# GpSimd's decay of the last two heads' state over 120 partitions instead of 80

## The chip, the cores and the metric

The kernel runs on one core of a Trainium2 chip. The metric is the device time of one execution in microseconds (us). A core has five engines that run side by side, each through its own list of instructions in order: TensorE (PE in the profile, with PEld for its weight loads), VectorE (DVE), ScalarE (ACT), GpSimd (POOL) and SyncE (SP, which here only issues transfers). On-chip memory (SBUF) has 128 partitions, and an instruction works on the same stretch of each partition that it covers. "80x82" in the profile means 80 partitions with 82 elements in each.

## What is computed

Two parts, one after the other. First a recurrent attention (an mLSTM cell) over 4 batches, 8 heads, 768 steps and head width 40, with a matrix state C and a vector state n for each head:

```python
m_new = np.maximum(f_gate[:, :, t] + m, i_gate[:, :, t])
f_stab = np.exp(f_gate[:, :, t] + m - m_new)
i_stab = np.exp(i_gate[:, :, t] - m_new)
C = f_stab * C + i_stab * outer(vt, kt)
n = f_stab * n + i_stab * kt
y[:, :, t] = sigmoid(o_gate) * (C @ qt) / max(|n . qt|, 1)
```

Then a gated feed-forward on the 3072 rows of 320 numbers that come out: `(sigmoid(x @ w_gate) * (x @ w_val)) @ w_out`, with an inner width of 1536. All data are float32.

## The kernel before

**Units.** The 768 steps are cut into 6 chunks of 128. A unit n = 4c + b is one chunk c of one batch b; there are 24. A unit loads q, k, v and the output gate, turns q and k, computes scores inside the chunk (L749 and its like), multiplies them by a matrix of decays (L868), sums over the values (L929, from unit 8 on with the decays split into three bfloat16 parts, L883 and L887 on GpSimd), and adds what the state of the chunks before gives (matmul L913, scaled at L918).

**The state.** `cst` holds C and n of all heads between chunks: 128 partitions, then batch, then 3 groups of heads, then 123 columns. Groups 0 and 1 hold three heads each (3 x 40 = 120 partitions, 3 x 41 = 123 columns); group 2 holds the last two heads (80 partitions, 82 columns). After a chunk, `cd` multiplies the state by the chunk's decay (L1039, on GpSimd), `cm` brings the chunk's own sum from PSUM to a temporary tile (L1056, ScalarE), and `ca` adds that to the state (L1061, VectorE). Each of the three is there twice for a unit: `.0` for groups 0 and 1 together (120x246) and `.1` for group 2 (80x82). `cd` and `ca` exist for chunks 1 to 4, so 16 of each form run. `cdec` holds the decays, with one value for each partition, chunk, batch and group. For chunk 0, `cm` writes into `cst` itself.

**The feed-forward** is cut into 103 pieces: matmuls into two PSUM tiles pg (L1080, L1084, L1085), tanh on ScalarE (L1090, `th`), gate times value on VectorE (L1097, `gx`), a split of the result into two parts (L1102 on ScalarE, L1107 on VectorE), and the output matmuls (L1117 to L1119). These pieces are mixed with the units so that TensorE has work throughout.

**What sets the order.** The list ORDER (L46 to L192) names every operation once; they are issued in that order, and each engine takes its own in that order. Waits between engines are semaphores that the framework puts in. So an engine whose next instruction can't go on holds back all that are behind it in its list.

**GpSimd's other work** around the change: L659 (a difference of decays, 128x1024), L667 (a causal mask, `affine_select`, 128x1024), L883 and L887 (the splits), L877 (k times decay), L896 and L901 (the split of v), L1018 (the low part of x). At the start it clears and fills constant tiles (L331 to L354, and the identity). VectorE's instructions with two inputs in SBUF are `ca` (L1061), `sl` (L729, on stacks of q and k, 126x1024), L976 and L527; those of L1097, L1107, L918 and L941 have one input in PSUM.

Of the kernel before, what the change touches and what calls it, by code (L numbers as in the profile page):

```python
# [13 lines left out]
ALU = mybir.AluOpType  # L14
# [29 lines left out]


ORDER = """  # L46
    lo0 wz il lf i1 wdo0 li lq0 wdv0 lk0 tab pz wdr0 wao0 i0 lk1 og0 i3 i2 ga lq1 gm0 gb sp1.1 sp0.1 tap wav0 wbo0
    wco0 woo0 gs0 war0 tr0.1 wk0 tac cp0.1 wbr0 sp1.0 tr0.0 ee1.1 sp0.0 wdo4 gc lk2 wcr0 wbv0 wk1 wk2 lv0 ld2 tr1.0
    lv1 ee0.1 cp0.0 tr1.1 ee0.0 wk3 cp1.0 lq2 wk4 l10 wdg0 wor0 s0.0 wk5 kw0 gm1 wcv0 whr0 wov0 gm2 cp1.1 t0.1 s1.0
    t0.0 who0 wk6 tr2.1 wlr0 av0 l11 gm3 ee1.0 whv0 kw1 t1.1 wlo0 t1.0 lo1 tr2.0 cp2.1 nd0 av1 ns0 cs0 wdo1 ee2.0  # L50
    ee2.1 lq3 ro0 ld3 wk7 wao4 wlv0 cp2.0 nd1 xd0 xt0 wk8 wag0 wbg0 og1 wao1 ns1 xh0 em2 cm0.1 wcg0 ro1 lv2 kw2 wm
    lk3 wbo4 xl0 wog0 xd1 wbo1 cm0.0 wco4 whg0 wdg1 xt1 wco1 xh1 tr3.0 cp3.0 woo4 xl1 u1.0 woo1 wdo3 ee3.1 lo2 gm4
    s2.0 wlg0 t2.0 wdv1 u0.0 who4 wlo4 ee3.0 t2.1 tr3.1 r1.0 cp3.1 tbp lo3 em3 kw3 wag1 wk9 wao3 i8 wbg1 cs1 wdr1
    gs1 cm1.0 tbc wk10 og2 r0.0 l12 wbo3 wk11 wcg1 lk4 who1 av2 wco3 th0 wog1 woo3 gx0 u0.1 whg1 cm1.1 ns2 lv3 wlo1
    r0.1 gh0 nd2 gl0 s3.0 wlg1 wav1 og3 dn0.1 u1.1 wbv1 who3 wcv1 t3.0 wdo5 wov1 war1 lq4 wbr1 ro2 wlo3 lo4 th1 r1.1
    u0.2 dn0.0 wcr1 whv1 wao5 l13 t3.1 gx1 gh1 wor1 wbo5 cs2 wlv1 ld4 av3 wdo2 gm5 whr1 gl1 nd3 cm2.1 dn1.1 cm2.0
    u1.2 ns3 gd wdv3 xd2 tr4.0 xt2 wlr1 wco5 ro3 woo5 r0.2 cp4.0 xd3 xh2 th2 r1.2 tr4.1 wdo10 gx2 dn1.0 xl2 cp4.1
    ee4.1 lq5 u0.3 xt3 gh2 wao2 gl2 og4 wbo2 xh3 r0.3 wdg2 tdp wco2 woo2 th3 i7 who5 xl3 tdc who2 lk5 wlo5 u1.3 r1.3
    wav3 wlo2 gx3 u0.4 tr4.2 r0.4 cs3 th4 cp4.2 dn2.1 gh3 u0.5 wao10 wbv3 gl3 wbo10 u1.4 wco10 dn2.0 ld5 lq6 qb4.1
    wdr2 r1.4 ee4.0 tr5.0 qb4.0 r0.5 wag2 gx4 cm3.1 dn3.0 em4 th5 kw4 dn3.1 gh4 woo10 gl4 wcv3 cm3.0 wov3 who10  # L60
    qb4.2 wbg2 wdv2 u0.6 u1.5 r1.5 dn4.3 cp5.0 whv3 gx5 s4.2 r0.6 wlv3 gh5 t4.2 th6 wdr3 lv4 gl5 in4 s4.0 wcg2 u1.6
    war2 ti4 r1.6 wbr2 wdg3 u0.7 dn4.2 gx6 t4.0 lo6 wlo10 l14 r0.7 wcr2 i6 wav2 gh6 wog2 whg2 wlg2 s4.1 wor2 gl6
    wdg4 cs4 dn5.3 u1.7 wdr4 whr2 r1.7 wlr2 th7 ee5.1 wbv2 wcv2 dn5.2 gx7 t4.1 war3 dn6.3 ee5.0 wbr3 wov2 whv2 gh7
    u0.8 wlv2 wcr3 wor3 av4 gl7 wag3 ld6 r0.8 em5 lk6 u1.8 r1.8 cm4.1 dn7.3 th8 wbg3 og6 cm4.0 ad4 wcg3 tr5.2 war4
    nd4 lv5 ns4 tr6.0 lo7 whr3 cp5.2 dn6.2 wbr4 u0.9 dn7.2 wlr3 tr5.1 gx8 gh8 cp6.0 ee6.1 wdo6 tr6.2 r0.9 gl8 wcr4
    ro4 wor4 qb5.0 wao6 cp5.1 l15 dn8.2 wog3 lv6 wbo6 lq7 u1.9 whg3 cp6.2 tep qb5.2 wlg3 dn8.1 wco6 tr6.1 r1.9 dn8.3
    tec th9 whr4 wdv4 s5.0 cp6.1 gx9 wag4 kw5 gh9 u0.10 qb6.0 wdr5 wbg4 lk7 cd4.1 wcg4 qb5.1 wlr4 gl9 t5.0 in5 ca4.1
    war5 u1.10 r1.10 ti5 cd4.0 ee6.0 dn9.1 r0.10 woo6 wog4 wbr5 th10 dn8.0 dn9.3 lq9 wcr5 s5.1 who6 wlo6 whg4 gx10
    u0.11 wdo8 gh10 wdv5 wav4 wor5 gl10 wbv4 wcv4 dn9.2 t5.1 xd4 qb6.2 wlg4 u1.11 whr5 s5.2 dn10.1 r0.11 em6 th11
    dn10.0 lv7 wov4 t5.2 wlr5 gs2 wdo7 wao8 dn9.0 tr7.0 wao7 whv4 dn10.2 r1.11 wbo8 wlv4 ld7 lo5 u0.12 wco8 gx11  # L70
    gh11 gs3 wbo7 av5 cp7.0 lq8 cs5 gl11 woo8 wav5 ca4.0 og5 ee7.1 dn10.3 wdg5 wbv5 lv8 kw6 u1.12 cm5.1 wco7 cm5.0
    ad5 ns5 who8 nd5 s6.2 woo7 gs5 xt4 wcv5 t6.2 og7 ro5 wlo8 gs4 xh4 r0.12 r1.12 in6 th12 lk8 u0.13 who7 wag5 xl4
    wdo9 qb6.1 wdo11 gx12 xd5 wlo7 wbg5 l17 dn11.1 tr7.2 ti6 gh12 r0.13 cd6.0 tr7.1 dn11.0 wcg5 gl12 wov5 cp7.2
    dn11.2 th13 s6.1 cp7.1 dn12.3 wog5 wao9 whg5 wlg5 l18 s6.0 u1.13 qb7.2 cd5.0 l16 tq8 lq10 whv5 r1.13 cd5.1 u0.14
    gx13 t6.0 ca5.1 t6.1 dn12.1 ca5.0 dn11.3 wlv5 ld8 wbo9 r0.14 dn12.0 wco9 gh13 tw8.0 av6 woo9 tw8.3 dn12.2 gl13
    wao11 who9 ad6 qb7.0 cs6 nd6 th14 wlo9 tw8.1 ee7.0 dn13.0 u1.14 r1.14 ns6 dn13.2 cm6.1 wbo11 gx14 xt5 ld9 gh14
# [127 lines left out]
def mlstm_then_gated_ffn_kernel(  # L204
# [13 lines left out]
    nc = tc.nc  # L218
    B, H, S, D = q.shape
# [7 lines left out]
    DA = D + 1  # L227
# [5 lines left out]
    def E(name, n=None):  # L233
        x = PARAM["eng"].get(name if n is None else f"{name}{n}", PARAM["eng"].get(name, "p"))
        return nc.gpsimd if x == "p" else nc.vector
# [18 lines left out]
    def sbt(tag, shape, dt, name, bufs=1):  # L254
        return sb.tile(shape, dt, tag=turn(tag, bufs), name=name)
# [6 lines left out]
    def op(name):  # L262
        def put(f):
            assert name not in ops, name
            ops[name] = f
            return f
        return put
# [19 lines left out]
    cdec = const.tile([P, NCH, B, 3], F32, name="cdec")  # L287
    cst = const.tile([P, B, 3, 3 * DA], F32, name="cst")
# [6 lines left out]
    @op("wz")  # L295
    def _():
        nc.vector.memset(warm, 0.0)
# [31 lines left out]
    @op("i0")  # L329
    def _():  # L330
        nc.gpsimd.memset(mend[:, 0:1], -1e30)  # L331
        nc.gpsimd.memset(m0, 0.0)

    @op("i1")
    def _():
# [234 lines left out]
    def unit(n):  # L570
        c, b = divmod(n, B)
        t0 = c * L
# [9 lines left out]
        def rows(t):  # L582
            return t[b, :, t0 : t0 + L, :].rearrange("h t d -> t h d")
# [4 lines left out]
        @op(f"lq{n}")  # L588
        def _():
            qt[n] = pads[n][0][:, :, :D] if padded else sbt("q", [P, H, D], F32, f"q_{n}", 3)  # L590
            (nc.scalar if n == 0 else nc.sync).dma_start(qt[n], rows(q))
# [179 lines left out]
        elif not stacked:  # L771
            hl = "hl"[b % 2]

            for g, (h0, nh) in enumerate(GROUPS):
                r = nh * D
# [29 lines left out]
        else:  # L805
            for g, (h0, nh) in enumerate(GROUPS):
                r = nh * D
# [224 lines left out]
        for y, (g0, ng, r, w) in enumerate(((0, 2, 3 * D, 3 * DA), (2, 1, 2 * D, 2 * DA))):  # L1032
            gs = slice(g0, g0 + ng)
            cv = cst[:r, b, gs, :w]

            if c > 0:
                @op(f"cd{n}.{y}")
                def _(cv=cv, gs=gs, r=r, ng=ng, w=w, y=y):
                    E(f"cd{y}", n).tensor_tensor(cv, cv, cdec[:r, c, b, gs].unsqueeze(2).broadcast_to([r, ng, w]), ALU.mult)  # L1039

            if c > 0 and PARAM["CA"]:
                @op(f"ca{n}.{y}")
                def _(cv=cv, gs=gs, r=r, w=w):
                    for j in range(w // DA):
                        js = slice(j * DA, (j + 1) * DA)
                        nc.vector.scalar_tensor_tensor(cv[:, :, js], pc_[n][:r, gs, js], rmask[:r, j : j + 1], cv[:, :, js],
                                                       ALU.mult, ALU.add)
                continue

            @op(f"cm{n}.{y}")  # L1050
            def _(cv=cv, gs=gs, r=r, ng=ng, w=w, y=y):
                tmp = cv if c == 0 else sbt(f"ct{ng}", [P, ng, w], F32, f"ct{ng}_{n}")[:r]
                tmps[y] = tmp
                for j in range(w // DA):
                    js = slice(j * DA, (j + 1) * DA)
                    nc.scalar.activation(tmp[:, :, js], pc_[n][:r, gs, js], AF.Copy, scale=rmask[:r, j : j + 1])  # L1056

            if c > 0:
                @op(f"ca{n}.{y}")
                def _(cv=cv, y=y):  # L1060
                    E("ca", n).tensor_tensor(cv, cv, tmps[y], ALU.add)  # L1061
# [70 lines left out]
    n = 0  # L1132
# [39 lines left out]
```

## Time and profile before

| what | us |
|---|---|
| median of 3 runs | 537.78 |
| lowest and highest of them | 537.2, 539.06 |
| the profiled execution, its own time | 535.29 |
| its span, from the first to the last instruction | 533.6 |
| TensorE busy | 509.8 (96% of the span) |
| VectorE busy | 360.3 (68%) |
| ScalarE busy | 250.6 (47%) |
| GpSimd busy | 240.4 (45%) |

The profile is of one execution. The difference between its own time and its span (1.7 us) lies around the instructions. TensorE's clock was granted in full throughout. Busy shares are means over the whole span: GpSimd's 45% says nothing about whether somebody waits for it in a given stretch. In the rows further down, a line starts with the time of the start and the duration in us; a bracket at its end holds how long the engine sat idle before it and what ended that.

### The profile page before, as it was taken

How to read it: one execution, taken by the hardware profiler on the slowest of the kernel's cores; microseconds unless marked ns; L12 is line 12 of the kernel's file. 1: busy time of each engine (PE TensorE's matmuls, PEld its weight loads, DVE VectorE, ACT ScalarE, POOL GpSimd, SP SyncE). 2: the span in 40 equal slices, each digit the busy share in tenths (PEclk: the TensorE clock that was granted, in tenths of full speed). 3: DMA queues.
4: the chain of work that ended last, by engine and by line, in shares of the span. 5: the costliest groups of instructions: out<-in, count | busy, mean ns of one | idle time of the engine just before them, and what ended most of it. 6: DMA issues, size and time to landing. Idle time of an engine off the chain costs nothing.

```text
span 533.6 us, 10378 instructions
## 1 busy us (share of the span) xinstructions
PE 509.8 (96%) x3637; PEld 465.4 (87%) x3637; DVE 360.3 (68%) x827; ACT 250.6 (47%) x576; POOL 240.4 (45%) x268
## 2 busy tenths in 40 slices
PE   5999999999998998899999889999999999999997
PEld 5889988889998998888888778888788888999996
DVE  6998889867586887667688288857555475753322
ACT  4878766645435454453436352544424333323222
POOL 1566567556508754267546564645350605130000
PEclk9999999999999999999999999999999999999999
DMA  9898887554969777698768775765794515101001
GB/s 214 209 244 242 220 182 202 138 119 97 180 153 197 133 141 145 144 204 184 139 127 196 144 161 135 163 127 125 143 206 86 129 31 136 39 28 41 1 1 50
DMA packets 222476, 74.13 MB, mean 139 GB/s; under 512 B 167380, under 2 KB 214168, under 8 KB 222424
## 3 DMA queue, kind: packets, MB, share of 16 engines
q1 hardware_dynamic: 221336, 73.20, 61.9%
q8 instruction: 29, 0.48, 0.4%
q10 hardware_dynamic: 1088, 0.26, 0.3%
q14 instruction: 23, 0.19, 0.1%
HBM read 61.54 MB, written 11.90 MB: 138 GB/s over the span
## 4 chain that ended last, share of the span: by engine, by line
PE 80%; DMA 8%; DVE 5%; SPq 2%; issue 2%; ACT 1%; POOL 0%; DVEq 0%; ACTq 0%
PE pg L1080 34%; PE po L1117 7%; PE po L1119 6%; PE po L1118 6%; PE pg L1084 6%; PE pg L1085 5%; DMA qs<-scq 3%; PE av L947 3%; PE s L749 2%; PE av L929 2%; PE in L913 2%; DMA scx<-tx 2%; PE cs L1028 2%; PE s L804 1%; DMA xf<-scx 1%
## 5 line engine op out<-in xcount | busy, mean ns | idle before, releaser
L1080 PE MATMUL pg<-xh,wh 128*128 128x256 f32 (+1 forms) x412 | 107.0, 341 | 12.9 <-DVE gl L1107 6.7
L1102 ACT ACTIVATE gh<-pg 128x256 fp32r<-128x256 f32 (+1 forms) x103 | 48.3, 469 | 139.1 <-DVE pg L1097 91.5
L1097 DVE SCALAR_TENSOR_TENSOR pg<-sg,pg 128x256 f32<-128x256 f32 (+1 forms) x103 | 54.8, 532 | 82.7 <-PE pg L1085 54.3
L1080 PE MATMUL pg<-xl,wh 128*128 128x256 f32 (+1 forms) x412 | 101.3, 327 | 0.6 <-POOL xl L1018 0.6
L1080 PE MATMUL pg<-xh,wl 128*128 128x256 f32 (+1 forms) x412 | 101.0, 326 | 0.0
L1117 PE MATMUL po<-oh,gh 128*128 128x320 f32 x288 | 92.4, 321 | 0.1
L1119 PE MATMUL po<-oh,gl 128*128 128x320 f32 x288 | 89.6, 311 | 0.2 <-DVE gl L1107 0.2
L1118 PE MATMUL po<-ol,gh 128*128 128x320 f32 x288 | 89.3, 310 | 0.0
L1080 PEld LDWEIGHTS pg<-xh,wh 128*128 128x128 f32 x412 | 66.8, 189 | 20.3 <-DVE gl L1107 9.3
L1107 DVE TENSOR_TENSOR gl<-pg,gh 128x256 fp32r<-128x256 f32 (+1 forms) x103 | 54.2, 526 | 40.5 <-ACT gh L1102 39.3
L1090 ACT ACTIVATE sg<-pg 128x256 f32<-128x256 f32 (+1 forms) x103 | 48.1, 467 | 64.7 <-PE pg L1085 58.3
L1080 PEld LDWEIGHTS pg<-xl,wh 128*128 128x128 f32 x412 | 68.9, 189 | 8.5 <-POOL xl L1018 1.4
L1080 PEld LDWEIGHTS pg<-xh,wl 128*128 128x128 f32 x412 | 68.9, 189 | 7.2
L883 POOL TENSOR_TENSOR dr<-d 128x1024 f32<-128x1024 f32 x16 | 30.4, 1903 | 97.5 <-DVE d L868 71.9
L1084 PE MATMUL pg<-xh,w 128*128 128x256 f32 (+1 forms) x206 | 69.9, 340 | 0.0
L1085 PE MATMUL pg<-xl,w 128*128 128x256 f32 (+1 forms) x206 | 66.9, 326 | 0.0
L1117 PEld LDWEIGHTS po<-oh,gh 128*128 128x128 f32 x288 | 54.4, 189 | 3.8 <-ACT gh L1102 0.4
L1118 PEld LDWEIGHTS po<-ol,gh 128*128 128x128 f32 x288 | 54.2, 188 | 3.4
L1119 PEld LDWEIGHTS po<-oh,gl 128*128 128x128 f32 x288 | 54.2, 188 | 0.8 <-DVE gl L1107 0.7
L1018 POOL TENSOR_TENSOR xl<-xf,xh 128x384 fp32r<-128x384 f32 x16 | 16.9, 1056 | 56.9 <-ACT xh L1014 49.0
L1085 PEld LDWEIGHTS pg<-xl,w 128*128 128x128 f32 x206 | 39.1, 190 | 2.1
L1084 PEld LDWEIGHTS pg<-xh,w 128*128 128x128 f32 x206 | 39.0, 189 | 2.2
(156 smaller groups left out, 914.8 us busy)
## 6 DMA issues: line engine op xcount, KB each, us to landing
d<-mscr SPq DMA_DIRECT2D x22, 512.0 KB
ks<-scq SPq DMA_DIRECT2D x48, 168.0 KB
qs<-scq SPq DMA_DIRECT2D x48, 168.0 KB
scq<-tq SPq DMA_DIRECT2D x64, 80.0 KB
o<-in_o_gate_dram SPq DMA_DIRECT2D x24, 160.0 KB
su_o<-in_moe_w_out_dram SPq DMA_DIRECT2D x12, 320.0 KB
v<-in_v_dram SPq DMA_DIRECT2D x24, 160.0 KB
out_dram<-ob SPq DMA_DIRECT2D x24, 160.0 KB
```

What stands on the lines that cost most here:

```text
L883: E("da", n).tensor_tensor(dr[n][0], dm[n], top(dm[n]), ALU.subtract)
L1018: (E("xl", n) if xbounced else nc.vector).tensor_tensor(xl[c][:, :, bs], xf[n], xh[c][:, :, bs].bitcast(F32), ALU.subtract)
L1080: nc.tensor.matmul(p, w[y][:, a, fs], x[c][:, a, n0:n1], start=(i + a == 0), stop=False)
L1084: nc.tensor.matmul(pg[n, y], w2[y][:, fs], xh[c][:, 2, n0:n1], start=False, stop=False)
L1085: nc.tensor.matmul(pg[n, y], w2[y][:, fs], xl[c][:, 2, n0:n1], start=False, stop=True)
L1090: nc.scalar.activation(s, pg[n, 0], AF.Tanh, scale=0.5)
L1097: nc.vector.scalar_tensor_tensor(sgs[n], gate, 1.0, pg[n, 1], ALU.add, ALU.mult)
L1102: nc.scalar.activation(ghs[n][:, :nt], sgs[n], AF.Copy)
L1107: E("gl", n).tensor_tensor(gls[n][:, :nt], sgs[n], ghs[n][:, :nt].bitcast(F32), ALU.subtract)
L1117: nc.tensor.matmul(p, ghs[n][:, ts], oh[:, j, :], start=(j == 0), stop=False)
L1118: nc.tensor.matmul(p, ghs[n][:, ts], ol[:, j, :], start=False, stop=False)
L1119: nc.tensor.matmul(p, gls[n][:, ts], oh[:, j, :], start=False, stop=(j == NF - 1))
```

## The change

A new operation `iz` on GpSimd clears partitions 64 to 127 of group 2 in `cst`, for all four batches, once at the start. And `cd`, the decay, works on 120 partitions in both its forms; before, the form of group 2 worked on the 80 that hold data. The rows 80 to 119 of group 2 hold zeros, are multiplied by a decay of zero, and nobody reads them. ORDER gets the name `iz` behind `i0`; its lines are wrapped anew and nothing else in it moves.

```diff
-    lo0 wz il lf i1 wdo0 li lq0 wdv0 lk0 tab pz wdr0 wao0 i0 lk1 og0 i3 i2 ga lq1 gm0 gb sp1.1 sp0.1 tap wav0 wbo0
+    lo0 wz il lf i1 wdo0 li lq0 wdv0 lk0 tab pz wdr0 wao0 i0 iz lk1 og0 i3 i2 ga lq1 gm0 gb sp1.1 sp0.1 tap wav0
...
         nc.gpsimd.memset(mend[:, 0:1], -1e30)
         nc.gpsimd.memset(m0, 0.0)
 
+    @op("iz")
+    def _():
+        nc.gpsimd.memset(cst[64:, :, 2, : 2 * DA], 0.0)
+
...
             if c > 0:
                 @op(f"cd{n}.{y}")
-                def _(cv=cv, gs=gs, r=r, ng=ng, w=w, y=y):
-                    E(f"cd{y}", n).tensor_tensor(cv, cv, cdec[:r, c, b, gs].unsqueeze(2).broadcast_to([r, ng, w]), ALU.mult)
+                def _(gs=gs, ng=ng, w=w, y=y):
+                    cw = cst[: 3 * D, b, gs, :w]
+                    E(f"cd{y}", n).tensor_tensor(cw, cw, cdec[: 3 * D, c, b, gs].unsqueeze(2).broadcast_to([3 * D, ng, w]), ALU.mult)
```

## Rows read from the trace of the kernel before

**Rows 1.** The two forms of L1039 on POOL: busy us, mean ns, idle before.

```profile
L1039 POOL TENSOR_TENSOR cst<-cst,cdec 120x246 f32<-120x246 f32 x16 | 10.7, 667 | 0.1
L1039 POOL TENSOR_TENSOR cst<-cst,cdec 80x82 f32<-80x82 f32 x16 | 5.6, 352 | 7.3 <-PE in L913 7.3
```

**Rows 2.** Timeline of PE, 163 to 176 and 308 to 325 us: its two longest stops.

```profile
173.46 0.50 PE L1080 MATMUL pg<-xh,wh 128*128 128x256 f32 x2 [1.69 <-DVE gl L1107]
...
321.15 0.73 PE L1080 MATMUL pg<-xh,wh 128*128 128x512 f32 x2 [2.79 <-ACT sg L1090]
```

**Rows 3.** The chain that ended last, 160 to 178 and 305 to 325 us: start, us, what.

```profile
169.98 2.13 DVE qs L729
...
318.12 1.27 DVE ks L729
```

**Rows 4.** Timeline of POOL, 308 to 325 us, and its next instruction after that.

```profile
311.65 0.32 POOL L1039 TENSOR_TENSOR cst<-cst,cdec 80x82 f32<-80x82 f32 x1 [1.89 <-PE in L913]
311.93 2.14 POOL L667 TENSOR_SCALAR_AFFINE_SELECT d<-d 128x1024 f32<-128x1024 f32 x2
314.03 1.90 POOL L887 TENSOR_TENSOR ds<-dr 128x1024 bf16<-128x1024 f32 x1
...
316.49 1.44 POOL L877 TENSOR_TENSOR k<-k,d 128x320 f32<-128x320 f32 x2
...
326.61 1.90 POOL L883 TENSOR_TENSOR dr<-d 128x1024 f32<-128x1024 f32 x1 [8.68 <-PE av L929]
```

**Rows 5.** Timeline of DVE, 308 to 325 us: the add of the state, twice.

```profile
312.46 5.74 DVE L1061 TENSOR_TENSOR cst<-cst,ct 120x246 f32<-120x246 f32 x1
...
322.23 0.40 DVE L1061 TENSOR_TENSOR cst<-cst,ct 120x246 f32<-120x246 f32 x1
```

**Rows 6.** Timeline of POOL, 163 to 176 us.

```profile
167.67 0.32 POOL L1039 TENSOR_TENSOR cst<-cst,cdec 80x82 f32<-80x82 f32 x1
167.94 1.09 POOL L667 TENSOR_SCALAR_AFFINE_SELECT d<-d 128x1024 f32<-128x1024 f32 x1
...
170.30 0.73 POOL L896 TENSOR_TENSOR vs<-v 128x328 f32<-128x328 f32 x1
175.20 1.27 POOL L667 TENSOR_SCALAR_AFFINE_SELECT d<-d 128x1024 f32<-128x1024 f32 x1 [4.17 <-ACT d L663]
```

**Rows 7.** Timeline of DVE, 163 to 176 us: L729, twice.

```profile
168.63 3.48 DVE L729 SCALAR_TENSOR_TENSOR qs<-qs,rsign,qt 126x1024 fp32r<-126x1024 f32 x1
...
174.24 1.28 DVE L729 SCALAR_TENSOR_TENSOR ks<-ks,rsign,kt 126x1024 fp32r<-126x1024 f32 x1
```

**Rows 8.** Timeline of POOL, then of DVE, 199 to 212 us.

```profile
203.13 0.32 POOL L1039 TENSOR_TENSOR cst<-cst,cdec 80x82 f32<-80x82 f32 x1
203.41 0.74 POOL L877 TENSOR_TENSOR k<-k,d 128x320 f32<-128x320 f32 x1
...
202.97 1.27 DVE L1061 TENSOR_TENSOR cst<-cst,ct 80x82 f32<-80x82 f32 x1
207.72 0.51 DVE L695 STREAM_TRANSPOSE tq<-k 128x320 f32<-128x320 f32 x1 [1.63 <-DMA k<-in_k_dram]
```

**Rows 9.** Timeline of POOL, then of DVE, 224 to 229 us.

```profile
225.64 1.90 POOL L883 TENSOR_TENSOR dr<-d 128x1024 f32<-128x1024 f32 x1
227.49 0.77 POOL L1039 TENSOR_TENSOR cst<-cst,cdec 120x246 f32<-120x246 f32 x1
...
226.57 1.24 DVE L1061 TENSOR_TENSOR cst<-cst,ct 120x246 f32<-120x246 f32 x1
```

**Rows 10.** Start: timeline of POOL, then of PE.

```profile
1.32 0.62 POOL L336 MEMSET mg<- 32x640 f32 x1
...
6.06 2.08 PE L622 MATMUL mb<-m,ident 128*128 128x128 f32 x8 [2.03 <-DVE m L423]
```

**Rows 11.** Busy us of each engine in two stretches (PE, PEld, DVE, ACT, POOL).

```profile
173.40:318.40 145.00, 137.85 (x988) 125.14 (x988) 102.02 (x231) 67.05 (x144) 81.54 (x82) 1.00 0.77 158
321.10:529.80 208.70, 206.16 (x1434) 188.55 (x1434) 116.72 (x277) 74.03 (x148) 65.67 (x56) 1.00 0.42 91
```

More of the change, by code (lines that the diff above doesn't have):

```diff
@@ L46 @@
 ORDER = """
-    lo0 wz il lf i1 wdo0 li lq0 wdv0 lk0 tab pz wdr0 wao0 i0 lk1 og0 i3 i2 ga lq1 gm0 gb sp1.1 sp0.1 tap wav0 wbo0
[L48 to L71, printed above, removed]
@@ L72 @@
-    ad5 ns5 who8 nd5 s6.2 woo7 gs5 xt4 wcv5 t6.2 og7 ro5 wlo8 gs4 xh4 r0.12 r1.12 in6 th12 lk8 u0.13 who7 wag5 xl4
-    wdo9 qb6.1 wdo11 gx12 xd5 wlo7 wbg5 l17 dn11.1 tr7.2 ti6 gh12 r0.13 cd6.0 tr7.1 dn11.0 wcg5 gl12 wov5 cp7.2
+    lo0 wz il lf i1 wdo0 li lq0 wdv0 lk0 tab pz wdr0 wao0 i0 iz lk1 og0 i3 i2 ga lq1 gm0 gb sp1.1 sp0.1 tap wav0
+    wbo0 wco0 woo0 gs0 war0 tr0.1 wk0 tac cp0.1 wbr0 sp1.0 tr0.0 ee1.1 sp0.0 wdo4 gc lk2 wcr0 wbv0 wk1 wk2 lv0 ld2
+    tr1.0 lv1 ee0.1 cp0.0 tr1.1 ee0.0 wk3 cp1.0 lq2 wk4 l10 wdg0 wor0 s0.0 wk5 kw0 gm1 wcv0 whr0 wov0 gm2 cp1.1 t0.1
@@ new lines @@
+    s1.0 t0.0 who0 wk6 tr2.1 wlr0 av0 l11 gm3 ee1.0 whv0 kw1 t1.1 wlo0 t1.0 lo1 tr2.0 cp2.1 nd0 av1 ns0 cs0 wdo1
+    ee2.0 ee2.1 lq3 ro0 ld3 wk7 wao4 wlv0 cp2.0 nd1 xd0 xt0 wk8 wag0 wbg0 og1 wao1 ns1 xh0 em2 cm0.1 wcg0 ro1 lv2
+    kw2 wm lk3 wbo4 xl0 wog0 xd1 wbo1 cm0.0 wco4 whg0 wdg1 xt1 wco1 xh1 tr3.0 cp3.0 woo4 xl1 u1.0 woo1 wdo3 ee3.1
+    lo2 gm4 s2.0 wlg0 t2.0 wdv1 u0.0 who4 wlo4 ee3.0 t2.1 tr3.1 r1.0 cp3.1 tbp lo3 em3 kw3 wag1 wk9 wao3 i8 wbg1 cs1
+    wdr1 gs1 cm1.0 tbc wk10 og2 r0.0 l12 wbo3 wk11 wcg1 lk4 who1 av2 wco3 th0 wog1 woo3 gx0 u0.1 whg1 cm1.1 ns2 lv3
@@ new lines @@
+    wlo1 r0.1 gh0 nd2 gl0 s3.0 wlg1 wav1 og3 dn0.1 u1.1 wbv1 who3 wcv1 t3.0 wdo5 wov1 war1 lq4 wbr1 ro2 wlo3 lo4 th1
+    r1.1 u0.2 dn0.0 wcr1 whv1 wao5 l13 t3.1 gx1 gh1 wor1 wbo5 cs2 wlv1 ld4 av3 wdo2 gm5 whr1 gl1 nd3 cm2.1 dn1.1
+    cm2.0 u1.2 ns3 gd wdv3 xd2 tr4.0 xt2 wlr1 wco5 ro3 woo5 r0.2 cp4.0 xd3 xh2 th2 r1.2 tr4.1 wdo10 gx2 dn1.0 xl2
+    cp4.1 ee4.1 lq5 u0.3 xt3 gh2 wao2 gl2 og4 wbo2 xh3 r0.3 wdg2 tdp wco2 woo2 th3 i7 who5 xl3 tdc who2 lk5 wlo5
+    u1.3 r1.3 wav3 wlo2 gx3 u0.4 tr4.2 r0.4 cs3 th4 cp4.2 dn2.1 gh3 u0.5 wao10 wbv3 gl3 wbo10 u1.4 wco10 dn2.0 ld5
@@ new lines @@
+    lq6 qb4.1 wdr2 r1.4 ee4.0 tr5.0 qb4.0 r0.5 wag2 gx4 cm3.1 dn3.0 em4 th5 kw4 dn3.1 gh4 woo10 gl4 wcv3 cm3.0 wov3
+    who10 qb4.2 wbg2 wdv2 u0.6 u1.5 r1.5 dn4.3 cp5.0 whv3 gx5 s4.2 r0.6 wlv3 gh5 t4.2 th6 wdr3 lv4 gl5 in4 s4.0 wcg2
+    u1.6 war2 ti4 r1.6 wbr2 wdg3 u0.7 dn4.2 gx6 t4.0 lo6 wlo10 l14 r0.7 wcr2 i6 wav2 gh6 wog2 whg2 wlg2 s4.1 wor2
+    gl6 wdg4 cs4 dn5.3 u1.7 wdr4 whr2 r1.7 wlr2 th7 ee5.1 wbv2 wcv2 dn5.2 gx7 t4.1 war3 dn6.3 ee5.0 wbr3 wov2 whv2
+    gh7 u0.8 wlv2 wcr3 wor3 av4 gl7 wag3 ld6 r0.8 em5 lk6 u1.8 r1.8 cm4.1 dn7.3 th8 wbg3 og6 cm4.0 ad4 wcg3 tr5.2
@@ new lines @@
+    war4 nd4 lv5 ns4 tr6.0 lo7 whr3 cp5.2 dn6.2 wbr4 u0.9 dn7.2 wlr3 tr5.1 gx8 gh8 cp6.0 ee6.1 wdo6 tr6.2 r0.9 gl8
+    wcr4 ro4 wor4 qb5.0 wao6 cp5.1 l15 dn8.2 wog3 lv6 wbo6 lq7 u1.9 whg3 cp6.2 tep qb5.2 wlg3 dn8.1 wco6 tr6.1 r1.9
+    dn8.3 tec th9 whr4 wdv4 s5.0 cp6.1 gx9 wag4 kw5 gh9 u0.10 qb6.0 wdr5 wbg4 lk7 cd4.1 wcg4 qb5.1 wlr4 gl9 t5.0 in5
+    ca4.1 war5 u1.10 r1.10 ti5 cd4.0 ee6.0 dn9.1 r0.10 woo6 wog4 wbr5 th10 dn8.0 dn9.3 lq9 wcr5 s5.1 who6 wlo6 whg4
+    gx10 u0.11 wdo8 gh10 wdv5 wav4 wor5 gl10 wbv4 wcv4 dn9.2 t5.1 xd4 qb6.2 wlg4 u1.11 whr5 s5.2 dn10.1 r0.11 em6
@@ L74 @@
+    th11 dn10.0 lv7 wov4 t5.2 wlr5 gs2 wdo7 wao8 dn9.0 tr7.0 wao7 whv4 dn10.2 r1.11 wbo8 wlv4 ld7 lo5 u0.12 wco8
+    gx11 gh11 gs3 wbo7 av5 cp7.0 lq8 cs5 gl11 woo8 wav5 ca4.0 og5 ee7.1 dn10.3 wdg5 wbv5 lv8 kw6 u1.12 cm5.1 wco7
+    cm5.0 ad5 ns5 who8 nd5 s6.2 woo7 gs5 xt4 wcv5 t6.2 og7 ro5 wlo8 gs4 xh4 r0.12 r1.12 in6 th12 lk8 u0.13 who7 wag5
+    xl4 wdo9 qb6.1 wdo11 gx12 xd5 wlo7 wbg5 l17 dn11.1 tr7.2 ti6 gh12 r0.13 cd6.0 tr7.1 dn11.0 wcg5 gl12 wov5 cp7.2
     dn11.2 th13 s6.1 cp7.1 dn12.3 wog5 wao9 whg5 wlg5 l18 s6.0 u1.13 qb7.2 cd5.0 l16 tq8 lq10 whv5 r1.13 cd5.1 u0.14
```

## The prediction, made before the changed kernel ran

> **What bounds the kernel now.** The busy shares come first: TensorE works for 96% of the span, so only its stops can be won, and they are few. The timeline of PE shows where they are. Outside the start the two longest are one of 1.69 us before 173.46 and one of 2.79 us before 321.15 [rows 2]. The chain that ended last names what stood in the way: both times VectorE's L729 [rows 3], which has two inputs in SBUF. GpSimd hardly appears in that chain, so at first sight a change to one of its operations should do nothing. The reason to look further is the length of VectorE's instructions just before the stops. The add of the state, L1061, takes 0.40 us in one place and 5.74 in another, same form [rows 5]. L729 takes 1.28 and once 3.48 [rows 7]. Such an instruction was held, not working.
>
> What held it is seen by laying GpSimd's timeline beside it. The 5.74 less its 0.40 of work leaves 5.34 us of waiting, so work began at 317.80. GpSimd was in an unbroken run from 311.65 to 316.49 + 1.44 = 317.93 [rows 4]. The 3.48 less 1.28 leaves 2.20; work began at 170.83, and the run on GpSimd ended at 170.30 + 0.73 = 171.03 [rows 6]. In both cases VectorE got in when GpSimd had nothing left, 0.1 to 0.2 us before the recorded end, and was passed over at every border between two GpSimd instructions before that: at six in the second stretch, at four in the first.
>
> That isn't how it goes elsewhere. At 226.57 the same L1061 took 1.24 us, so it began at 227.41, just where the running GpSimd instruction ended (225.64 + 1.90 = 227.54), although the next one stood ready; that one then took 0.77 instead of its usual time, so it was GpSimd that waited [rows 9]. I find five such cases of a two-input VectorE instruction let in at the first border with GpSimd work queued behind it; one stands there. What sets the long holds apart: in each, an 80x82 decay (L1039) ran earlier in the same unbroken run [rows 4, 6]. A third case fits: L1061 in its smaller form took 1.27 us where an 80x82 decay came just behind its arrival, and was let in only at the end of the run, near 204.15 [rows 8]. Three of three with such a decay, none of five without.
>
> **The reading.** A GpSimd instruction over 80 partitions leaves the share of GpSimd that serves the last rows without work. If that share goes straight on to the next instruction, the parts are out of step by the decay's 0.32 us [rows 4, 6] until the queue runs dry, there is no moment between two instructions at which all of GpSimd lets go, and VectorE is passed over. The Trainium skill's GPSIMD Engine Reference, section 2.1, says as much of the parts: a core begins the next instruction once its own share of the last is done, though others still write; no run here has shown that apart from the holds above. With 120 partitions the parts stay in step.
>
> **The change part by part.**
>
> *The wider decay.* Sixteen instructions stay sixteen. 82 elements take 0.352 us on 80 partitions and 246 take 0.667 on 120 [rows 1]: time goes with the length, so I take no change. Bounds: nothing at all, and 0.667 − 0.352 = 0.32 us each if rows cost as much as length; GpSimd's idle time behind the two runs (4.17 and 8.68 us [rows 4, 6]) covers that.
>
> *The clear `iz`.* 328 elements on 64 partitions, once. It's shorter than the clear of 640 elements, 0.62 us [rows 10], which I take as the upper bound; the lower is nothing. It delays the identity that TensorE's first matmul reads, but TensorE then idles 2.03 us for VectorE's scan [rows 10], which covers it three times. Cost taken: nothing. ScalarE's first write of `cst`, much later, has one more producer to wait for, long done.
>
> *The first hold, at 168.63.* L667 ends at 167.94 + 1.09 = 169.03 [rows 6]; with the usual 0.15 us before that, L729 begins at 168.88 and ends at 170.16 instead of 172.11. What follows from L729's end to TensorE's restart took 173.46 − 172.11 = 1.35 us, so it could restart at 171.5; one hold of `ca` behind the 120x246 decay adds up to 0.6. TensorE was free at 173.46 − 1.69 = 171.77. Of the 1.69, between 1.3 and 1.7 goes; I take 1.5. The next limit is TensorE's own work.
>
> *The second hold, at 312.46.* The two L667 take 2.14 together [rows 4], so the first ends at 313.0; L1061 works from 312.87 to 313.27 instead of 318.20. L729 behind it comes up against the second L667, to 314.4 at most as that began 0.4 late. From L1061's end to TensorE's restart took 321.15 − 318.20 = 2.95, so now 314.4 + 2.95 = 317.35, while TensorE has work until 321.15 − 2.79 = 318.36. All 2.79 goes, with 1.0 to spare. GpSimd falls behind by 0.40 + 1.28 there, twice that if the other L729 gets in as well; it idled 8.68 us behind the run [rows 4].
>
> *The third, at 202.97.* VectorE waits 1.63 us for a transfer before 207.72 [rows 8]; what is won disappears there. Nothing.
>
> *Sum.* 1.5 + 2.8 = 4.3 us. Part can be given back: TensorE idles 145.0 − 137.85 = 7.15 us between the two stops, and 208.7 − 206.16 = 2.5 after the second [rows 11], partly at the end of transfers. Most transfers are issued after a wait for compute and so move along. I take off 0.3 as a middle between nothing and the whole 1.5 of the first stop. Gain 4.0: 535.3 to 531.3 for the profiled execution, whose own time lies 2.5 below the median of the runs shown (537.8), so against the median **533.8**.
>
> **A rule against this change.** The long holds of rows 4 to 7 went past several borders. The Trainium skill's SBUF — State Buffer, section "SBUF: two separate sides", says that VectorE and GpSimd share one pair of ports, given to whichever starts first, for one whole instruction. By that rule alone a hold lasts at most one GpSimd instruction, partitions don't matter, and the sum is 0. The rows agree for five cases and not for three.
>
> **Rivals.**
>
> *No change.* The holds have another cause than the 80 rows: VectorE loses whenever GpSimd's queue is full, or when it arrives during L667. Then the decay lasts 0.35 us as before, both stops stay, and the time is 537.8. For it: two of three holds began during L667 [rows 4 to 7]. Against it: the five cases let in with the queue full [rows 9], one of them out of an L667. Chance 0.13.
>
> *Spent at the next transfer.* The holds go, but the lead is lost in the 7.15 us of later stops: all of the first, half of the second; 1.4 remain, 536.4. Against it: the chain runs on through compute. Chance 0.08.
>
> *Slower: new collisions.* Each two-input VectorE instruction that arrives at the start of a 1.90-us GpSimd instruction [rows 4] is held that long even when all is well. With all times shifted, other L1061 and L729 meet L659, L883 and L887 on TensorE's path, between 173 and 425 us. Three more at 1.9 just pass the gain (5.7 − 4.5); with four it's 537.8 + 7.6 − 4.5 = 540.9. Against it: rows 9 show holds of 0.84 that cost TensorE little. Chance 0.05.
>
> **How the numbers follow.** The forecast has 0.74: 531.8 to 535.8 on its own, from 1.5 us more than the two stops (shifted collisions work both ways) to 2.0 of gain left. The range reaches up to no change: 531.8 to 537.9. Outside are the slower rival and the tails, 0.2. A measurement of this kernel tells some 0.3% (1.6 us) from no change. Faster by more than that: 0.74 + 0.03 of the second rival = 0.77. Within it: 0.13 + 0.05 = 0.18. Slower: 0.05.
>
> **What would show it.** Right: L1039 has 32 instructions over 120 partitions, the short form still near 0.32 to 0.35 us; no L1061 or L729 lasts over its work plus one GpSimd instruction (1.9 us), so L1061's longest falls from 5.74 to 2.3 or less and L729's 3.48 to 3.2 or less; TensorE's stops of 1.69 and 2.79 shrink to a few tenths; TensorE's idle time in the two stretches of rows 11 is about as before. Wrong: holds past several borders in runs without an 80-row instruction, which would refute the reading; or the holds gone and TensorE idle as long elsewhere, which would leave the reading and refute the sum.

## The result and the profile after

| | us |
|---|---|
| changed kernel, median of 4 runs | 530.17 (529.84 to 531.09) |
| kernel before, median of 4 runs | 537.49 (534.41 to 539.06) |
| ratio, 95% interval | 0.9874, 0.9827 to 0.992 |
| profiled execution, its own time | 530.45 (before 535.29) |
| its span | 528.7 (before 533.6) |

The changed kernel is faster by 1.3%; the medians lie 7.3 us apart. Forecast were a gain of 4.0 us and a time of 533.8; the measured time lies below the range. Between the two profiled executions the difference is 4.8 us. That 7.3 and 4.8 differ is the main thing that the experiments had to explain. Here and below, a ratio rests on the executions within 1.5% of their kernel's fastest, a median on all of them, so a ratio need not be the quotient of the two medians.

The profile of the changed kernel (span, then busy time of each engine):

```profile
span 528.7 us, 10379 instructions
...
PE 510.3 (97%) x3637; PEld 465.7 (88%) x3637; DVE 355.2 (67%) x827; ACT 250.7 (47%) x576; POOL 243.5 (46%) x269
```

TensorE and ScalarE do the same work in the same time. VectorE's busy time fell by 5.1 us (360.3 before) and GpSimd's rose by 3.1 (240.4 before). Busy time in a trace includes time in which an instruction is held; part of the waiting has changed sides.

The groups on GpSimd that the diff touches (line numbers are 4 or 5 higher than before):

```profile
L1044 POOL TENSOR_TENSOR cst<-cst,cdec 120x246 f32<-120x246 f32 x16 | 10.3, 642 | 0.1
L1044 POOL TENSOR_TENSOR cst<-cst,cdec 120x82 f32<-120x82 f32 x16 | 5.3, 331 | 7.3 <-PE in L917 7.3
L336 POOL MEMSET cst<- 64x328 f32 x1 | 0.4, 372 | 0.1
```

The decay over 120 partitions takes 331 ns, over 80 it took 352 [rows 1]: the 40 rows more cost nothing. The clear takes 0.37 us, once.

The stretch of the long hold, timeline of GpSimd and of VectorE, 306 to 322 us; these answer to [rows 4, 5]:

```profile
310.20 0.32 POOL L1044 TENSOR_TENSOR cst<-cst,cdec 120x82 f32<-120x82 f32 x1 [1.90 <-PE in L917]
310.48 2.31 POOL L671 TENSOR_SCALAR_AFFINE_SELECT d<-d 128x1024 f32<-128x1024 f32 x2
312.76 2.86 POOL L891 TENSOR_TENSOR ds<-dr 128x1024 bf16<-128x1024 f32 x1
...
316.18 2.64 POOL L881 TENSOR_TENSOR k<-k,d 128x320 f32<-128x320 f32 x2
...
311.01 0.83 DVE L1066 TENSOR_TENSOR cst<-cst,ct 120x246 f32<-120x246 f32 x1
312.12 1.74 DVE L733 SCALAR_TENSOR_TENSOR ks<-ks,rsign,kt 126x1024 fp32r<-126x1024 f32 x1 [0.28 <-ACT kt L727]
```

The same instructions in the same order, and the add of the state takes 0.83 us where it took 5.74. It is held for 0.83 - 0.40 = 0.43, up to the end of the first of the two L671. GpSimd now waits in its turn: its L891 takes 2.86 instead of 1.90, the two L881 2.64 instead of 1.44. TensorE's stop of 2.79 us behind it [rows 2] is gone altogether. The first hold, timeline of VectorE and of TensorE, 163 to 176 us, beside [rows 7, 2]:

```profile
169.13 1.73 DVE L733 SCALAR_TENSOR_TENSOR qs<-qs,rsign,qt 126x1024 fp32r<-126x1024 f32 x1
...
172.42 0.51 PE L1085 MATMUL pg<-xh,wh 128*128 128x256 f32 x2 [0.33 <-DVE gl L1112]
```

L733 takes 1.73 instead of 3.48, and the stop is 0.33 instead of 1.69. These two were not the two longest stops outside the start, as the prediction and [rows 2] call them. The trace of the kernel before has a longer one than the first between them:

```profile
208.60 0.50 PE L1080 MATMUL pg<-xh,wh 128*128 128x256 f32 x2 [2.34 <-DVE gl L1107]
```

The change doesn't reach it; in the changed kernel it is there with 1.54 us, and with 1.78 and 2.48 in its two later profiles. Last, the stretches between and behind the two places, beside [rows 11]:

```profile
172.40:316.00 143.60, 137.07 (x983) 124.50 (x984) 99.19 (x233) 67.33 (x146) 81.21 (x80) 1.00 0.77 160
316.00:524.90 208.90, 206.78 (x1440) 189.17 (x1439) 118.72 (x277) 74.55 (x148) 67.50 (x59) 1.00 0.42 91
```

TensorE idles 6.5 us in the first and 2.1 in the second, where it was 7.15 and 2.5. The idle time there is what the first number of a line (the length) leaves when TensorE's busy time, the second, is taken off. Nothing of the lead was given back; a little came on top.

### The profile page after: what moved, and what is told of

Read it like the earlier page. It is cut to its first block, busy times and chain, and to the rows that moved or that the text cites. A ratio compares the mean times of both kernels' runs of the same rounds, so it can differ in the third digit from the quotient of the medians.

```text
span 528.7 us, 10379 instructions
## 1 busy us (share of the span) xinstructions
PE 510.3 (97%) x3637; PEld 465.7 (88%) x3637; DVE 355.2 (67%) x827; ACT 250.7 (47%) x576; POOL 243.5 (46%) x269
## 4 chain that ended last, share of the span: by engine, by line
PE 52%; DMA 7%; DVE 2%; issue 2%; SPq 2%; ACT 1%; POOL 0%; DVEq 0%; ACTq 0%
PE pg L1085 24%; PE po L1122 5%; PE po L1124 5%; PE po L1123 5%; PE pg L1089 4%; PE pg L1090 4%; DMA qs<-scq 2%; PE av L933 2%; PE s L753 2%; DMA scx<-tx 2%; PE in L917 1%; DMA xf<-scx 1%; SPq L680 1%; DVE gl L1112 1%; DMA k<-in_k_dram 1%
```

## The experiments

Times are medians, each beside the kernel before on the same chip; the kernel before itself differs between the four sets (537.11 to 540.85), so ratios are compared across sets, not microseconds.

| run | this, us (range) | before, us | ratio, 95% interval |
|---|---|---|---|
| 112 rows | 540.92 (537.38 to 543.16) | 540.85 | 1.004, 0.998 to 1.01 |
| 113 rows | 534.02 (531.0 to 535.13) | 540.85 | 0.9909, 0.9857 to 0.9961 |
| the clear alone | 539.94 (536.8 to 543.6) | 540.85 | 1.0032, 0.9973 to 1.0091 |
| before, again | 537.58 (534.87 to 543.54) | 540.85 | 0.9978, 0.9923 to 1.0033 |
| changed, again | 531.26 (530.11 to 532.07) | 537.49 | 0.9868, 0.9839 to 0.9897 |
| 80 rows and a wait | 533.98 (532.89 to 536.35) | 537.49 | 0.9913, 0.9881 to 0.9945 |
| 48 clears on VectorE | 545.53 (542.02 to 545.67) | 537.49 | 1.0121, 1.0086 to 1.0157 |
| tq12 later | 533.18 (530.95 to 539.49) | 537.49 | 0.9896, 0.9861 to 0.9932 |
| unit 16 alone on 80 | 535.77 (532.68 to 540.56) | 537.11 | 0.9982, 0.9942 to 1.0023 |
| units 8 and 9 alone on 80 | 531.21 (530.24 to 534.21) | 537.11 | 0.9896, 0.985 to 0.9941 |
| 23 clears on VectorE | 537.48 (533.07 to 539.84) | 537.11 | 0.9991, 0.9959 to 1.0024 |
| tq11 later | 530.48 (527.57 to 531.13) | 537.11 | 0.9859, 0.9811 to 0.9908 |
| tq13 later | 530.15 (527.72 to 531.88) | 538.03 | 0.9853, 0.9809 to 0.9896 |
| changed, third time | 528.82 (527.63 to 531.76) | 538.03 | 0.9842, 0.9803 to 0.9881 |

### One row more: 112 and 113

```diff
-                    cw = cst[: 3 * D, b, gs, :w]
+                    rr = 3 * D if y == 0 else 112
+                    cw = cst[:rr, b, gs, :w]
...
```

(and `else 113` in the second).

> The changed kernel with the short form of the decay on 112 partitions instead of 120 (rows 80 to 111 are the zeros; 112 to 119 are left out, and nothing reads them). Theory of parts out of step: GpSimd serves its partitions in eight shares of 16, so 112 rows leave the last share without work just as 80 left three. VectorE's long holds come back: at least one L1066 or L733 is held past more than one border of GpSimd instructions, TensorE gets back stops of 1.5 us or more before 175 and before 325 us, and the time is that of the kernel before, 534 to 539 us. Rival 'the width of 80 as such, or a tail of rows in the middle of the tile': 112 is nearly 120, so the time is that of the changed kernel, 530 to 531 us, and no hold lasts over one GpSimd instruction (1.9 us).

> The changed kernel with the short form of the decay on 113 partitions: one row more than its sister experiment with 112. Theory of parts out of step: that one row gives the last share its work, and it takes as long over one row as over sixteen; no hold goes past a border, L1066 lasts 1.3 us at most, the time is 529.8 to 531.1 us as for 120 rows, some 7 us below the run with 112. Rival 'every missing row costs alike': no difference between 112 and 113 that can be measured (under 1 us).

Timelines of GpSimd and VectorE with 112 rows, 308 to 322 us:

```profile
312.32 0.32 POOL L1045 TENSOR_TENSOR cst<-cst,cdec 112x82 f32<-112x82 f32 x1 [1.87 <-PE in L917]
...
313.12 5.74 DVE L1067 TENSOR_TENSOR cst<-cst,ct 120x246 f32<-120x246 f32 x1
```

And with 113:

```profile
311.00 0.32 POOL L1045 TENSOR_TENSOR cst<-cst,cdec 113x82 f32<-113x82 f32 x1 [1.87 <-PE in L917]
...
311.81 0.83 DVE L1067 TENSOR_TENSOR cst<-cst,ct 120x246 f32<-120x246 f32 x1
```

The decay itself takes 0.32 us either way; one row in it decides between a hold of 5.34 us in VectorE and one of 0.43, and between the time of the kernel before and that of the changed one. The Trainium skill's GPSIMD Engine Reference, section 1, gives each GpSimd core 16 partitions: 112 is seven cores' worth, 113 touches the eighth. The runs agree with that: a rule that counts rows would not set 112 apart from 113. The difference between the two, 6.9 us, is the one expected; both medians lie 2 to 3 us above the ranges given, and the kernel before, too, is 3 us slower in that set than in the first runs. Both rivals fell.

### The clear alone, and the kernel before again

```diff
+        nc.gpsimd.memset(cst[64:, :, 2, : 2 * DA], 0.0)
...
```

with the decay on 80 rows, as before.

> Only the clear at the start; the decay back on 80 partitions. Theory: the clear is worth nothing (TensorE's first matmul starts 0.5 us later, the wait for VectorE's scan behind it is shorter by as much), the long holds are there, 534 to 539 us. Rival 'the gain comes from the start or from another placement of the waits': a time near 530 us.

It's worth nothing that can be measured (1.0032, the interval holds 1), and its profile has the hold of 5.74 us. It even has one that the other profiles lack: L980 (x from o and den, two inputs in SBUF) takes 1.94 us from 289.65 on, where 0.49 is usual. An 80x82 decay ran before it in the same unbroken run of GpSimd; it is passed over at one border and begins at 291.10, 0.15 before that run ends.

The second run is the kernel before, unchanged.

> The kernel before, unchanged, for a second profile of it and more of its times. The forecast took the 4.0 us from one profiled execution at 535.3 and left the 2.5 us by which the median lies above that alone. If those 2.5 are long holds too, which differ from execution to execution: this profile shows held instructions that are not the three of the first profile (or other lengths), and the higher an execution's time the more us of holds past a border it has; times spread over 534 to 539 again while the changed kernel's stay within 1.5 us. If instead the 2.5 have another cause (transfers, the clock, the host): the same two stops of TensorE with the same lengths, whatever the time.

The first answer fell: its profile shows the same L1061 of 5.74 us and L729 of 3.26, with stops of 2.78 and 1.64. The runs with 112 rows and with the clear alone show the long hold too (5.74, a stop of 2.77), and in the first place stops of 1.25 and 1.63. The long hold doesn't differ between executions. What differs is what follows it. Busy time by stretches in the run with 112 rows (the stop, 10 us behind it, 10 more; the third number from the end is the granted clock of TensorE, as a share of full speed):

```profile
319.00:321.70 2.70, 0.03 (x1) 0.00 (x0) 2.70 (x4) 1.21 (x5) 0.00 (x0) 0.90 0.21 37
321.80:331.80 10.00, 9.99 (x48) 8.27 (x49) 5.14 (x11) 0.44 (x1) 0.26 (x1) 0.52 0.39 83
332.00:342.00 10.00, 10.00 (x75) 8.80 (x74) 8.28 (x31) 4.61 (x7) 7.51 (x7) 1.00 0.84 203
```

And in the first profile of the kernel before:

```profile
318.40:321.10 2.70, 0.00 (x0) 0.00 (x0) 2.70 (x4) 1.21 (x5) 0.00 (x0) 1.00 0.05 9
321.20:331.20 10.00, 10.00 (x75) 8.88 (x76) 8.49 (x25) 2.33 (x5) 4.51 (x3) 1.00 0.58 149
```

Behind the same stop the clock was at half (0.52 over 10 us, that is 1.2 of 2.4 GHz nearly throughout) in one execution and full in the other. TensorE is "busy" in both, but starts 48 matmuls instead of 75. Ten us at 0.52 are 4.8 us of full clock lost. Below, such a stretch is called a lapse. The run with the clear alone has the same stretch (0.52 over 9.8 us). The profile that the forecast was built on is one in which the clock held.

### One hold at a time

```diff
-                    cw = cst[: 3 * D, b, gs, :w]
+                    rr = 2 * D if y == 1 and n in (16,) else 3 * D
+                    cw = cst[:rr, b, gs, :w]
...
```

> The changed kernel with the decay of one single unit (16) back on 80 partitions, the one ahead of the hold of 5.34 us; the other fifteen stay on 120. Theory: that hold alone comes back, with its stop of 2.8 us near 318 to 322 us, and with it, in part of the executions, TensorE's clock at half for 10 us behind it, worth 5 us: a median 3 to 8 us above the changed kernel (530 to 531), so 533 to 539, and a spread of 4 us or more. By the forecast's own sum it is worth 2.8 and no more: 533 to 534 with a spread of 2.

(and `n in (8, 9)` for the other.)

> The changed kernel with the decays of units 8 and 9 alone back on 80 partitions, those ahead of the hold of 2.20 us. Theory: a hold of L733 of 1.5 to 2.2 us and TensorE's stop of 1.2 to 1.7 us near 174 come back, the clock doesn't follow a stop that short (no profile shows a lapse there): 1 to 2 us above the changed kernel, 531 to 533, spread 2 us. If the stops' cost is the clock alone: no difference.

VectorE and TensorE with unit 16 alone on 80 rows:

```profile
311.91 5.74 DVE L1067 TENSOR_TENSOR cst<-cst,ct 120x246 f32<-120x246 f32 x1
...
320.60 0.73 PE L1086 MATMUL pg<-xh,wh 128*128 128x512 f32 x2 [2.78 <-ACT sg L1096]
```

And with units 8 and 9:

```profile
169.03 2.83 DVE L733 SCALAR_TENSOR_TENSOR qs<-qs,rsign,qt 126x1024 fp32r<-126x1024 f32 x1
...
173.20 0.51 PE L1086 MATMUL pg<-xh,wh 128*128 128x256 f32 x2 [1.21 <-DVE gl L1113]
```

Each decay brings back its own hold and its own stop, and not the other's. One instruction of 0.32 us on 80 rows takes back almost the whole gain: 0.9982 beside 0.9842 to 0.9874 for the changed kernel, some 6 us of 537, twice the length of its stop (the intervals reach about 2 us to either side), and the times of the 12 runs spread over 7.9 us. The forecast's own sum (533 to 534, a spread of 2) fell. The other two decays cost little (0.9896; the interval overlaps the changed kernel's).

### The same hold from another cause

```diff
+    held = const.tile([P, 96], F32, name="held")
+    @op("hz")
+    def _():
+        for _ in range(48):
+            nc.vector.memset(held, 0.0)
...
-    ca15.0 r0.58 ...
+    hz ca15.0 r0.58 ...
```

> The changed kernel with 48 clears of a small tile on VectorE, some 5 us, right before the add of the state that was held for 5.34 us before. No 80-row decay. Theory: the price of that hold is TensorE's stop of 2.8 us behind it and, in some executions, TensorE's clock: in two of four profiles of held kernels it was at half (0.50) for some 10 us behind that very stop, and at full in the other two. So the stop of 2 to 3 us is back near 320 us, and the times spread over 4 to 7 us: 533 to 539, near 533 where the clock stayed and 538 or more where it fell. Rival 'the clock falls for another reason than the stop': all times within 1.5 us of each other, 3 us above the changed kernel.

The 48 clears took 10.71 us, twice what was meant; the stop was 8.07 us, and the clock fell in all five executions (means of 0.987 to 0.991). The size was a miss; the next run has `range(23)`.

> As the run with 48 clears on VectorE, with 23: those 48 took 10.71 us and not 5, so 23 should take 5.1. No 80-row decay anywhere. Theory: a stop of 2 to 3 us on TensorE near 320 us, the clock at half behind it in some executions: 533 to 540, a spread of 4 us or more, like the run with the decay of unit 16 alone on 80. If only the 80-row decay does that: within 1 us of the changed kernel plus the stop, 533 to 534.

Timelines of VectorE and of TensorE in that run:

```profile
310.13 5.09 DVE L343 MEMSET held<- 128x96 f32 x23
...
318.76 1.18 PE L1092 MATMUL pg<-xh,wh 128*128 128x512 f32 x2 [2.54 <-ACT sg L1102]
```

And three stretches of it, with the granted clock third from the end:

```profile
316.00:318.60 2.60, 0.23 (x2) 0.00 (x0) 2.60 (x4) 1.10 (x4) 0.00 (x0) 1.00 0.16 28
318.60:324.00 5.40, 5.24 (x20) 4.47 (x21) 2.67 (x5) 0.60 (x2) 0.00 (x0) 0.68 0.02 5
324.00:330.00 6.00, 6.00 (x56) 5.43 (x55) 5.72 (x20) 1.94 (x4) 4.15 (x3) 1.00 0.91 219
```

No 80-row decay is in this kernel. Five us of other work on VectorE at that place make a stop of 2.54, a lapse of the clock behind it (0.68 over 5.4 us), times from 533.07 to 539.84 and the time of the kernel before (ratio 0.9991). The answer "533 to 534" fell. So the price of the hold is the price of VectorE being late there: the stop and, in part of the executions, the clock.

### 80 rows, but no running ahead

```diff
+                    if y == 1:
+                        nc.gpsimd.tensor_copy(cst[:, b, 2, 3 * DA - 1 :], cst[:, b, 2, :1])
...
```

behind the decay, which is on 80 rows again.

> The decay of the last two heads on 80 partitions again, but right behind each of the 16 a copy of one element per partition on GpSimd that reads what the decay wrote and so waits until it has ended everywhere. The column that it writes is used by nobody. Theory of parts out of step: the wait brings the parts together again behind every 80-row decay, so the holds past a border vanish though the 80 rows stay, and the time is that of the changed kernel plus at most 1 us (16 copies of 0.1 to 0.3 us on GpSimd, mostly hidden): 530 to 535. Rival 'an 80-row decay itself is what VectorE loses against': the holds of 2 and 5 us stay, 536 to 541 us.

Timelines of GpSimd and of VectorE in that run, 309 to 322 us:

```profile
313.72 0.32 POOL L1045 TENSOR_TENSOR cst<-cst,cdec 80x82 f32<-80x82 f32 x1 [1.89 <-PE in L917]
314.11 0.18 POOL L1047 COPY cst<-cst 128x1 f32<-128x1 f32 x1
314.24 2.31 POOL L671 TENSOR_SCALAR_AFFINE_SELECT d<-d 128x1024 f32<-128x1024 f32 x2
...
314.53 1.07 DVE L1069 TENSOR_TENSOR cst<-cst,ct 120x246 f32<-120x246 f32 x1
```

The copy starts 0.07 us after the decay's end, while GpSimd's instructions otherwise start 0.04 before it: that's the wait. With 80 rows in place the add is held for 0.67 us, within one instruction, and no L1069, L733 or L980 of that profile is held past a border (the longest hold is 1.30). The add arrives at 314.53, behind the copy, so it isn't the gap of the wait that lets it in. So it isn't the 80 rows that VectorE loses against, it's what they leave behind in the queue. The kernel is 2.7 us slower than the changed one beside it, more than the 1 us expected; the 16 copies take 3.0 us of GpSimd. The profiled execution, the slowest of the six, has a stop of 2.68 us before 345.27 that the chain leads back to the transfer of d and not to a copy. Why the median is slower stays open.

### The stop that is left

A stop of 1.5 to 2.5 us stays near 207 us; TensorE waits there for a split on VectorE behind a pair of transposes. Three runs each moved one pair of transposes in ORDER to behind a split: tq12 behind gl32, tq11 behind gl26, tq13 behind gl37.

> The changed kernel with the operation tq12 (two transposes on VectorE, the second of which waits for the load of k) moved in ORDER behind gl32, for which TensorE stops 1.54 us at 206.75, the longest stop that is left. If that stop goes: 1 to 1.5 us below the changed kernel of this set, and less spread. If the lead is lost to the transfers behind it (tw12 is issued later): no difference within 0.5 us.

> The changed kernel with tq11 moved behind gl26 in ORDER (the run before moved tq12 and missed: the stop near 207 stayed). VectorE's second transpose of tq11 waits 1.6 to 2.6 us for the load of k, and the split that TensorE waits for stands behind it. Theory: the stop of 1.5 to 2.5 us near 207 goes, and the lapse of the clock behind it (0.58 to 0.60 in 208 to 212 us in two profiles): 1 to 3 us below the changed kernel, 527 to 530. If the lead is lost to the transfers: no difference within 0.5 us.

Both moved the wrong pair; the stop stayed (2.55 and 2.28 us), and nothing was gained (0.9896 and 0.9859). The right one is tq13, with the changed kernel beside it.

> The changed kernel with tq13 moved behind gl37 in ORDER. The runs with tq12 and tq11 moved left the stop near 207 us, since the transposes ahead of that split are tq13's (the add of the state that follows it there is unit 10's). Theory: the stop of 1.5 to 2.5 us near 207 shrinks to under 1 us, no clock under 0.97 in 204 to 212 us, the median 1 to 4 us below the changed kernel of this set. If the lead is lost to transfers behind it (the stops near 223 and 236 grow by as much) or a lapse never follows a stop there: within 0.5 us of the stop's length or no difference.

> The changed kernel once more, as the yardstick beside the run with tq13 moved. All theories: some 6 to 7 us below the kernel before; the stop near 207 of 1.5 to 2.5 us, with the clock lapsing behind it in some executions and not in others, so times spread over 1 to 3 us.

TensorE's timeline near 207 us with tq13 moved:

```profile
208.38 0.80 PE L1032 MATMUL cs<-v,k 128*120 128x123 f32 x6 [1.26 <-DVE den L969]
```

And in the changed kernel of that set:

```profile
207.28 0.51 PE L1085 MATMUL pg<-xh,wh 128*128 128x256 f32 x2 [1.78 <-DVE gl L1112]
```

The split now comes in time, and TensorE stops 1.1 us later for the next thing behind the transposes, which still wait for the load of k. No difference can be measured (0.9853 and 0.9842).

Neither of these two profiles shows a lapse near 207 us. Those of "changed, again" and tq12, with stops of 2.48 and 2.55, show 0.60 and 0.58 between 208 and 212 us; tq11, units 8 and 9, and the clear alone, with 2.28, 2.48 and 2.20, show 0.57 over 4 us. But 2.34 in the first profile of the kernel before, 2.33 with 112 rows and 2.18 with 113 rows were followed by full clock. In the run with unit 16 alone on 80, a stop of 1.80 before 223.81 was followed by a lapse, and its stop of 2.78 before 320.60 was not:

```profile
223.80:227.80 4.00, 3.99 (x20) 3.99 (x21) 2.40 (x4) 1.30 (x4) 4.00 (x5) 0.57 0.79 178
320.60:330.60 10.00, 10.00 (x75) 8.89 (x76) 8.50 (x25) 2.37 (x5) 4.47 (x3) 1.00 0.60 138
```

Two profiles (before, again; 80 rows and a wait) show a lapse near 304 us (0.65 and 0.81 from 300 to 304), where several short stops of up to 0.65 us stand close together and no long one; the first profile of the kernel before has such stops of up to 0.59 there and full clock. So a stop's length alone doesn't settle in these runs whether a lapse follows; what does stays open. No version was found that beats the changed kernel.

## Why the prediction was right, and where it was wrong

**The reading was right.** A GpSimd instruction that leaves a part of the engine without work lets VectorE be passed over until the queue runs dry. 112 against 113 rows shows that the part without work is the cause, the run with a wait shows that being out of step is, and the runs with one or two decays on 80 show that each hold belongs to the decay ahead of it. That parts run on ahead is inferred from these; no trace shows the parts singly. The Trainium skill's Perfetto Trace Analysis, section "GPSIMD Engine Instruction", says that each of the eight DSPs has its own queue and that this "*usually* doesn't matter in practice"; here it mattered by 1.3%. The signs named for "right" are there: the longest add of the state takes 1.24 us (2.3 were allowed), the longest L733 2.08 (3.2).

**The wider decay and the clear** cost nothing, as taken: 331 ns instead of 352, and 0.37 us in front of a wait. TensorE's first matmul began at 3.96 instead of 3.42 and the idle time behind it fell from 2.03 to 1.39 us.

**The holds came out as worked.** First: 1.5 us of its stop was to go, 1.36 went. Second: all 2.79 went, as worked out, and the hold of 0.41 that was worked out for the add measured 0.43. The rest of the working for the second place was wrong twice over without harm. It counted L729 twice: 314.4 is where L729 ends, and the 2.95 from L1061's end to TensorE's restart hold its 1.27 us once more. And L729 ended later than "314.4 at most": it waited 0.28 us for ScalarE and ended at 313.86, which is 315.3 in the times of the kernel before (GpSimd's decay starts 1.45 earlier here). The third place: the add takes 0.30 instead of 1.27, and VectorE waits for the load of k all the same, 1.55 us; no gain showed, as said.

**Given back.** 0.3 us were taken off. Instead TensorE's other idle time fell too, by 0.6 us between the places and 0.4 behind (6.5 for 7.15, 2.1 for 2.5). That is the smaller error: 4.8 us between the profiles instead of 4.0.

**The step that failed** is the last one of the sum, "whose own time lies 2.5 below the median of the runs shown (537.8), so against the median" 533.8. It carried the 2.5 us over as if they would stay. For the greater part they are what the change removes: the lapse of the clock behind the second stop, which the profiled execution happened not to have. In the 23 runs of the kernel before in the third set, the four with a mean granted clock of 0.999 or 1.0 took 533.8 to 534.5 us and the eight at 0.990 or below 539.4 to 540.9. In the same set tq11 later, which has the changed kernel's decays, took 527.6 to 530.7 in its three runs at 1.0: with the clock held on both sides some 5 us lie between them, about the 4.8 of the two profiles. The second stop's term, 2.8 us, was the length of the stop; alone it measured some 6 us in the median (unit 16 alone on 80), stop and lapse together.

The changed kernel keeps a stop of 1.5 to 2.5 us near 207, and behind it the clock lapsed for some 4 us in one of its three profiles. A lapse of 10 us was seen only behind the stop of 2.8. Its times spread over 1.3 to 4.1 us within a set. The clock isn't the whole of the spread. In the first set, three runs of the kernel before at 0.999 or 1.0 took 534.0 to 537.3 us and three with the clear alone at 1.0 took 536.8 to 539.6; what differs among those stays open.

**The rivals.** "No change" and "spent at the next transfer" fell with the result. "New collisions" fell too. The holds left in the changed profile last one GpSimd instruction each; the longest is 1.37 us, as before. Several are new or longer than before: L980 near 365 is held for 1.03 us where it was 0.31, and an L733 near 350 for 0.59 where it wasn't held. TensorE's idle time didn't grow.

## What to carry to other kernels

Give a GpSimd instruction in a dense queue work in all eight groups of 16 partitions, with rows of zeros if need be. Here they cost nothing (331 ns instead of 352), and a group left out held a VectorE instruction with two SBUF inputs over as many as seven GpSimd instructions. Tried were 80, 112, 113 and 120 rows. In a trace such a hold shows as one VectorE instruction far longer than its sisters that ends when GpSimd's queue runs dry; the cause stands earlier in that run and seems unrelated. And before summing savings from one profile, see where its time lies among the runs: what makes the other runs longer may hang on the same stop. The granted clock of the executions tells: it was 1.0 in the one that the forecast was built on, 0.986 to 0.990 in the eight slowest of the third set.

## What the runs showed of the hardware that wasn't expected

- TensorE's clock at half behind a stop of 2.8 us: 0.52 over 10 us in two executions, full in three (both profiles of the kernel before, and unit 16 alone on 80). Shorter lapses, of some 4 us, stood behind stops of 1.80 to 2.55 us in several profiles and were missing behind others as long. A lapse is not in the busy time and not in the waits, only in the granted clock of a stretch and in the number of matmuls started, 48 against 75.
- The release shows in the trace 0.13 us before the recorded end of the last GpSimd instruction of a run: 317.80 against 317.93 [rows 4, 5]. The Trainium skill's SBUF — State Buffer, section "SBUF: two separate sides", gives the shared pair to one instruction at a time; the runs say so only as long as all groups of GpSimd have work. With one group left out the hold went over six borders.
- 48 clears of 96 elements took 10.71 us, 0.22 each, as much as each of the eight clears of 192 elements at the start (1.67 us together). The 48 all write the same tile, the eight don't; whether that is why they are no shorter stays open.
